# Routing logits brought to token order by 32x32 transposes and four products with a repeated identity

## The chip, the core and the metric

The program runs on one core of one Trainium2 chip. Its engines work side by side and meet through semaphores: TensorE (PE in the rows, its weight loads PEld), VectorE (DVE), ScalarE (ACT), GpSimd (POOL) and SyncE (SP), which here only issues DMAs. The metric is the device time of one execution in microseconds; lower is better. Matrix products write to PSUM, an accumulation memory in banks of 512 fp32 columns on 128 partitions.

## What is computed

Three layers follow each other on a batch of 8 sequences with 576 tokens each. The change lies at the start of the third.

```python
def _attn_ref(q, k, v):              # 8 heads, head size 64, 32 landmarks (means of 18 rows)
    A = sm(q, k_lm); Bm = sm(q_lm, k_lm); C = sm(q_lm, k)
    Z = ...                          # 6 steps of 2 Z - Z Bm Z
    return A @ Z @ C @ v
def _moe_ref(x, w_in, w_out):        # 4608 x 512, 2048 wide
    r = np.maximum(x @ w_in, 0.0)
    return (r * r) @ w_out
def _moe2_ref(x, w_gate, w_output_gate, w1, w2):   # 8 experts, 1024 wide
    logits = x @ w_gate
    e_idx = np.argmax(logits, axis=1)
    probs = softmax(logits); gate_w = probs[arange(N), e_idx]
    eom = 1.0 / (1.0 + np.exp(-(x @ w_output_gate)))
    for e in range(8):
        mask = e_idx == e
        ye = np.maximum(x[mask] @ w1[e], 0.0) @ w2[e]
        out[mask] = gate_w[mask, None] * eom[mask, e, None] * ye
```

## The kernel before

A prologue computes the attention of batch 0 and turns the weights of the second layer into a split form. Then the second layer runs batch by batch (`gemm`), in two halves `c` of HC = 288 tokens. For each of 16 slices `f` of the 2048 hidden columns a hidden block `hp` is made by six products, ACT squares it into a high part `gh` and a square `g`, DVE takes the rest `gl` (`r`, `gh`, `g2`, `gl`, lines 1271 to 1277), and two slices later twelve products add it into four accumulators `acc` (`second`). There is one PSUM bank for `hp`. The attention of the next batch is woven into this stream in small steps (names `bank`, `two`, `x`, `aa`, `ec`, `mb`, `sums`, `st`). After all eight batches the experts of the third layer run (`experts`, names `xs`, `s`, `h`, `y`): in a main pass one expert per batch, the one most of its tokens chose; the other experts that any token chose follow in a loop (`others`).

Between the layers stands the routing, once per batch. `finish` sends the layer's output `x2` to memory and makes the logits. `self.wg` holds the 8 gate and 8 output-gate columns for each of four slices of 128 of the 512 channels, padded to 32. Four products, one per slice `m`, put partial logits into partitions 32m to 32m+31 of one bank `pl`, tokens along the free axis. DVE copies the bank into `lg` (128 partitions x 576 tokens, a half at a time, line 1353). `route` has two steps. `tokens` brings tokens to partitions: six products use 128 (once 64) columns of `lg` as weights and `self.sel` (four 16 x 16 identities stacked) as the moving operand, which adds the four partial sums on the way; five write 16 columns each for the token blocks t = 0 to 4, the sixth repeats the last 128 tokens, so that the 64 tokens of block 4 also stand on partitions 64 to 127. Three DVE copies take this to `L`. Small DVE operations find the largest logit (`oh`, one-hot), ACT takes two exponentials. `counts` multiplies `oh` with ones, in two products (blocks 0 to 3 on 128 partitions, block 4 on 64), to count the tokens of each expert, and derives `prim` and `flags`.

In fp32 each product shows in the trace as two passes: two rows of PE and two of PEld.

The order on each engine is set by a scheduler that simulates the program as it is built: it places every instruction where its model says it can run, with priorities, so a change of lengths moves instructions of other work too. What the code fixes are the calls `after(n, fn)`, which release a step n points of the main stream later, `run_of`, which ties the products of one step together (the products behind the first one get high priority), and `FENCED`, which holds the last logits behind the main stream. Lines 471 to 484 (`matmul`, `big`, `transpose`) are helpers: products of the woven steps appear under line 472 or 484, those of the main stream under 476, those called on the engine directly under their own line. In the prologue all appear under line 104.

Of the kernel before, what the change touches and what calls it, by code (L numbers as in the profile page):

```python
# [9 lines left out]
F32 = mybir.dt.float32  # L10
# [7 lines left out]
ALU = mybir.AluOpType  # L18
AX = mybir.AxisListType
# [3 lines left out]
B, H, S, D = 8, 8, 576, 64  # L23
LM = 32
# [3 lines left out]
NE = 8  # L28
# [4 lines left out]
HC = S // 2  # L33
KD = DM // 128
NFC = FF // 128
NT = (S + 127) // 128
NB = S // LM
# [40 lines left out]
def rows_of(t):  # L78
    return min(128, S - 128 * t)
# [42 lines left out]
class Kernel:  # L122
# [285 lines left out]
    def constants(self):  # L408
# [27 lines left out]
        self.sel = cst.tile([128, 16], F32, name="sel")  # L436
        for h in range(4):
            p = slice(32 * h, 32 * h + 32)
            nc.vector.tensor_copy(out=self.sel[p, :], in_=ident[p, 32 * h:32 * h + 16])
# [891 lines left out]
    def finish(self, b, c, x2):  # L1331
        nc = self.nc
        if c == 0:
            self.lg = self.rp.tile([128, S], F32, tag="lg", name="lg")
# [4 lines left out]
        def logits():  # L1339
# [13 lines left out]
            nc.vector.tensor_copy(out=lg[:, c * HC:(c + 1) * HC], in_=pl[:, 0:HC])  # L1353
# [6 lines left out]
    def route(self, b, lg):  # L1360
# [11 lines left out]
        def tokens():  # L1372
            pt = self.aux.tile([128, 512], F32, tag="b", name="pt")
            for t in range(NT):
                nc.tensor.matmul(  # L1375
                    pt[0:rows_of(t), 16 * t:16 * t + 16], lhsT=lg[:, 128 * t:128 * t + rows_of(t)], rhs=self.sel,
                    start=True, stop=True,
                )

            nc.tensor.matmul(pt[:, 16 * NT:16 * NT + 16], lhsT=lg[:, S - 128:S], rhs=self.sel, start=True, stop=True)  # L1380
            nc.vector.tensor_copy(out=L[64:128, NT - 1, :], in_=pt[64:128, 16 * NT:16 * NT + 16])
            nc.vector.tensor_copy(out=L[:, 0:NT - 1, :].rearrange("p t e -> p (t e)"), in_=pt[:, 0:16 * (NT - 1)])
            nc.vector.tensor_copy(out=L[0:64, NT - 1, :], in_=pt[0:64, 16 * (NT - 1):16 * NT])
# [14 lines left out]
        def counts():  # L1398
# [12 lines left out]
                pc[0:32, 0:NE * (NT - 1)], lhsT=self.ones, rhs=oh[:, 0:NT - 1].rearrange("p t e -> p (t e)"),  # L1411
                start=True, stop=True,
            )
            nc.tensor.matmul(
                pc[0:32, NE * (NT - 1):NE * NT], lhsT=self.ones[0:64, :], rhs=oh[0:64, NT - 1, :], start=True, stop=True
            )
            nc.vector.tensor_reduce(
                out=n[:, 0], in_=pc[0:32, 0:NE * NT].rearrange("p (t e) -> p e t", e=NE), axis=AX.X, op=ALU.add
            )
            nc.vector.tensor_reduce(out=s[:, 0:1], in_=n[:, 0], axis=AX.X, op=ALU.max)  # L1420
# [352 lines left out]
```

## Time and profile before

| quantity | value |
|---|---|
| time, median of 3 runs (lowest to highest) | 1255.96 us (1254.78 to 1258.02) |
| the profiled execution's own time | 1256.76 us |
| its span, first to last instruction | 1254.9 us |
| PE busy | 1217.9 us, 97% |
| DVE, ACT, POOL busy | 606.2, 611.0, 388.9 us |
| mean granted TensorE clock | 0.983 of full speed |

A timeline row reads: start, length, engine, line, operation, output tile <- input tiles, shape of the weights (partitions * columns), shape of the moving operand, and after x the number of passes merged into the row. Lengths of PE rows overlap, because passes are pipelined; what a pass costs the stream is the distance from its start to the start of what follows. The 1.9 us between time and span are outside the program's instructions.

### The profile page before, as it was taken

To read this page: it belongs to the slowest core of one execution; us is meant where nothing else is said; L and a number is where in the kernel's file an instruction comes from. 1 tells how busy PE (TensorE), PEld (TensorE's weight loads), DVE (VectorE), ACT (ScalarE), POOL (GpSimd) and SP (SyncE) were. 2 spreads that over 40 slices of the span, in tenths; PEclk is the share of its full clock that TensorE was granted. 3 is DMA by queue.
4 is the path that set the end of the run, shared out by engine and by line. 5 is a ranking of instruction groups with operands and counts; after the bars stand their busy time and mean duration, and the time that the engine had idled before them with its cause. 6 is when DMAs were issued, how large, how long until landed. Compare 5 with 4: busy or idle time off the path is not lost.

```text
span 1254.9 us, 25184 instructions
## 1 busy us (share of the span) xinstructions
PE 1217.9 (97%) x9886; PEld 1088.7 (87%) x9886; DVE 606.2 (48%) x1522; ACT 611.0 (49%) x1413; POOL 388.9 (31%) x516
## 2 busy tenths in 40 slices
PE   6889899999999999999999999999999999999996
PEld 4679788988988989989989999998898889888885
DVE  7893655755656555645745632234333323323231
ACT  6675355455455565465455454553343433424331
POOL 6540340612432240341341100153342423424220
PEclk8699899999999999999999999999999999999998
DMA  9963043142232142052041220152434435343231
GB/s 332 362 235 113 21 158 115 34 173 77 72 139 77 53 159 77 22 189 73 24 173 40 89 87 1 39 154 82 143 107 137 136 109 160 110 127 108 90 97 40
DMA packets 88408, 142.25 MB, mean 113 GB/s; under 512 B 6430, under 2 KB 61758, under 8 KB 84702
## 3 DMA queue, kind: packets, MB, share of 16 engines
q1 hardware_dynamic: 87854, 139.97, 34.2%
q8 instruction: 80, 1.31, 0.4%
q0 software_dynamic: 288, 0.43, 0.1%
q14 instruction: 42, 0.34, 0.1%
q10 hardware_dynamic: 144, 0.20, 0.0%
HBM read 117.47 MB, written 23.11 MB: 112 GB/s over the span
## 4 chain that ended last, share of the span: by engine, by line
PE 89%; DVE 6%; DMA 2%; ACT 2%; issue 1%; POOL 1%; POOLq 0%; ACTq 0%; DVEq 0%; SPq 0%
PE hp L476 31%; PE acc L476 30%; PE y L476 17%; PE two L472 3%; PE bank L472 2%; DVE x L577 1%; PE bank L484 1%; PE acc L104 1%; DVE sums L104 1%; DMA t<-in_k_dram 1%; PE pl L472 1%; PE bank L104 1%; DMA raw<-in_moe_w_in_dram 1%; PE pt L1375 1%; DMA raw<-in_moe_w_out_dram 0%
## 5 line engine op out<-in xcount | busy, mean ns | idle before, releaser
L476 PE MATMUL acc<-gl,hi 128*128 128x288 f32 x964 | 271.5, 299 | 3.1 <-DVE gl L104 1.6
L476 PE MATMUL acc<-gh,lo 128*128 128x288 f32 x964 | 267.9, 296 | 0.0
L476 PE MATMUL hp<-ab,gb 128*128 128x288 f32 x1434 | 240.3, 302 | 0.2
L476 PE MATMUL y<-s,h 128*128 128x512 f32 (+1 forms) x896 | 223.0, 396 | 0.8 <-ACT h L1518 0.5
L1277 DVE TENSOR_TENSOR gl<-g,gh 128x288 fp32r<-128x288 f32 x224 | 115.4, 516 | 218.0 <-ACT g L1276 216.3
L476 PEld LDWEIGHTS hp<-ab,gb 128*128 128x128 f32 x1434 | 202.1, 189 | 20.8 <-issue 14.7
L476 PEld LDWEIGHTS hp<-xs,s 128*128 128x128 f32 x1536 | 212.2, 188 | 7.4 <-DVE ls L1729 0.3
L476 PE MATMUL hp<-xs,s 128*128 128x288 f32 x1536 | 217.1, 295 | 0.2 <-DVE ls L1729 0.2
L1271 ACT ACTIVATE r<-hp 128x288 f32<-128x288 f32 x224 | 92.0, 411 | 229.0 <-PE hp L476 227.7
L476 PE MATMUL acc<-gh,hi 128*128 128x288 f32 x964 | 196.4, 300 | 0.1
L476 PEld LDWEIGHTS y<-s,h 128*128 128x128 f32 (+1 forms) x896 | 160.6, 184 | 37.7 <-ACT h L1518 0.7
L476 PEld LDWEIGHTS acc<-gl,hi 128*128 128x128 f32 x964 | 181.7, 188 | 10.5 <-DVE gl L1277 2.7
L476 PEld LDWEIGHTS acc<-gh,lo 128*128 128x128 f32 x964 | 181.5, 188 | 0.9 <-issue 0.9
L280 POOL TENSOR_TENSOR s<-r,s 128x256 fp32r<-128x256 f32 x128 | 101.9, 818 | 235.0 <-ACT s L268 234.9
L476 PEld LDWEIGHTS acc<-gh,hi 128*128 128x128 f32 x964 | 149.1, 188 | 18.8 <-ACT gh L1272 11.7
L1518 ACT ACTIVATE h<-hp 128x288 fp32r<-128x288 f32 x128 | 52.6, 411 | 189.0 <-PE hp L476 172.8
L1521 DVE SCALAR_TENSOR_TENSOR h<-hp,h 128x64 fp32r<-128x64 f32 (+2 forms) x192 | 62.6, 354 | 168.5 <-ACT h L1518 168.1
L268 ACT CAST s<-r 128x512 fp32r<-128x512 f32 x128 | 77.6, 617 | 69.3 <-PE y L476 56.3
L1272 ACT ACTIVATE gh<-r 128x288 fp32r<-128x288 f32 x224 | 99.5, 444 | 6.7 <-PE acc L476 0.2
L274 DVE TENSOR_TENSOR s<-r,s 128x512 fp32r<-128x512 f32 x64 | 50.7, 791 | 101.3 <-ACT s L268 101.3
L588 POOL COPY x<-x 32x576 f32<-32x576 f32 x48 | 32.7, 680 | 207.7 <-DVE x L577 108.3
L1276 ACT ACTIVATE g<-r 128x288 f32<-128x288 f32 x224 | 96.0, 429 | 0.0
(267 smaller groups left out, 1350.7 us busy)
## 6 DMA issues: line engine op xcount, KB each, us to landing
r<-in_moe_w_dram SPq DMA_DIRECT2D x128, 256.0 KB
wi<-win SPq DMA_DIRECT2D x28, 1024.0 KB
t<-in_k_dram SPq DMA_DIRECT2D x16, 576.0 KB
t<-in_q_dram SPq DMA_DIRECT2D x16, 576.0 KB
v<-in_v_dram SPq DMA_DIRECT2D x32, 288.0 KB
x_d<-x SPq DMA_DIRECT2D x16, 576.0 KB
xr<-x_d SPq DMA_DIRECT2D x16, 576.0 KB
raw<-in_moe_w_in_dram SPq DMA_DIRECT2D x16, 511.8 KB
```

The costliest lines, as they stand in the source:

```text
L104: return self.kernel.in_lane(self.name, fn(*args, **kw))
L268: hi = self.nc.scalar.copy(out=t[:, 0], in_=raw)
L274: lo_eng.tensor_tensor(out=t[:, 1], in0=raw, in1=t[:, 0].bitcast(F32), op=ALU.subtract)
L280: self.nc.gpsimd.tensor_tensor(out=out[:, p], in0=in0[:, p], in1=in1[:, p], op=op)
L472: self.in_run(lambda: self.nc.tensor.matmul(out, **kw))
L476: mm = self.nc.tensor.matmul(out, **kw)
L1271: nc.scalar.activation(out=r, in_=hp[:, 0:HC], func=ACTF.Relu)
L1272: nc.scalar.activation(out=gh, in_=r, func=ACTF.Square)
L1276: nc.scalar.activation(out=g2, in_=r, func=ACTF.Square)
L1277: nc.vector.tensor_tensor(out=gl, in0=g2, in1=gh.bitcast(F32), op=ALU.subtract)
L1518: nc.scalar.activation(out=h[:, t0:t1], in_=hp[:, 0:HC], func=ACTF.Relu)
L1521: nc.vector.scalar_tensor_tensor(out=h[:, to + a:to + z], in0=hp[:, a - t0:z - t0], scalar=0.0, in1=h[:, a:z].bitcast(F32), op0=ALU.max, o ...
```

## The change

The logits go into `lg` by a DVE transpose of 32 x 32 blocks instead of a copy, so that partition 32m + i of block n holds the 32 padded logit columns of token 32n + i, from channel slice m. Four products then have one and the same weight operand, `self.i32` (four 32 x 32 identities stacked), and stream `lg` with 80 columns each (5 blocks x 16 logits); product q writes the tokens of quarter q of each block of 128 to partitions 32q to 32q+31. They use column tiles of the array, as the four products of `pl` do. One DVE copy takes the result to `L`. `lg` grows to 20 blocks of 32; the last two, which no token fills, are set to zero by POOL once per batch, so that the 64 missing tokens choose expert 0. The counts are then one product over 128 partitions and 40 columns, and a new DVE operation subtracts the 64 (`self.extra`). `self.sel` and its four copies at the start are gone; two memsets of `extra` take their place.

```diff
--- before.py
+++ after.py
@@ -433,10 +433,9 @@
             nc.gpsimd.dma_start(
                 out=self.wg[:, :, NE * j:NE * (j + 1)], in_=w.rearrange("(k p) e -> p k e", p=128)
             )
-        self.sel = cst.tile([128, 16], F32, name="sel")
-        for h in range(4):
-            p = slice(32 * h, 32 * h + 32)
-            nc.vector.tensor_copy(out=self.sel[p, :], in_=ident[p, 32 * h:32 * h + 16])
+        self.extra = cst.tile([32, NE], F32, name="extra")
+        nc.vector.memset(self.extra, 0.0)
+        nc.vector.memset(self.extra[:, 0:1], float(128 * NT - S))
         self.dup = cst.tile([128, 2, D], F32, name="dup")
         for c in range(2):
             p = slice(D * c, D * c + D)
@@ -1331,7 +1330,8 @@
     def finish(self, b, c, x2):
         nc = self.nc
         if c == 0:
-            self.lg = self.rp.tile([128, S], F32, tag="lg", name="lg")
+            self.lg = self.rp.tile([128, NT * 4, LM], F32, tag="lg", name="lg")
+            nc.gpsimd.memset(self.lg[:, NB:], 0.0)
         lg = self.lg
         whole = (b, c) >= FENCED
         late = LOGITS_LATE if b < B - 1 else 2
@@ -1350,7 +1350,10 @@
                         self.follow(mm, e)
             if whole:
                 self.fence, self.fenced = mm, FENCE
-            nc.vector.tensor_copy(out=lg[:, c * HC:(c + 1) * HC], in_=pl[:, 0:HC])
+            n = NB // 2
+            nc.vector.transpose(
+                out=lg[:, n * c:n * c + n, :], in_=pl[:, 0:HC].rearrange("p (n l) -> p n l", l=LM)
+            )
 
         self.after(late, logits)
         if c == 1:
@@ -1371,16 +1374,14 @@
 
         def tokens():
             pt = self.aux.tile([128, 512], F32, tag="b", name="pt")
-            for t in range(NT):
-                nc.tensor.matmul(
-                    pt[0:rows_of(t), 16 * t:16 * t + 16], lhsT=lg[:, 128 * t:128 * t + rows_of(t)], rhs=self.sel,
-                    start=True, stop=True,
-                )
-
-            nc.tensor.matmul(pt[:, 16 * NT:16 * NT + 16], lhsT=lg[:, S - 128:S], rhs=self.sel, start=True, stop=True)
-            nc.vector.tensor_copy(out=L[64:128, NT - 1, :], in_=pt[64:128, 16 * NT:16 * NT + 16])
-            nc.vector.tensor_copy(out=L[:, 0:NT - 1, :].rearrange("p t e -> p (t e)"), in_=pt[:, 0:16 * (NT - 1)])
-            nc.vector.tensor_copy(out=L[0:64, NT - 1, :], in_=pt[0:64, 16 * (NT - 1):16 * NT])
+            with self.run_of():
+                for q in range(4):
+                    self.matmul(
+                        pt[32 * q:32 * q + 32, 0:16 * NT], lhsT=self.i32,
+                        rhs=lg.rearrange("p (t q) l -> p q t l", q=4)[:, q, :, 0:16], start=True, stop=True,
+                        tile_position=(0, 32 * q),
+                    )
+            nc.vector.tensor_copy(out=L.rearrange("p t e -> p (t e)"), in_=pt[:, 0:16 * NT])
             nc.vector.tensor_reduce(out=m[:, 0], in_=L[:, :, 0:NE], axis=AX.X, op=ALU.max)
             nc.vector.tensor_tensor(
                 out=lmx, in0=L[:, :, 0:NE], in1=m[:, 0].unsqueeze(2).to_broadcast(big), op=ALU.subtract
@@ -1408,15 +1409,12 @@
             self.after(2, lambda: nc.sync.dma_start(out=self.rt_d[b], in_=self.rt[:, b]))
             pc = self.aux.tile([128, 512], F32, tag="b", name="pc")
             nc.tensor.matmul(
-                pc[0:32, 0:NE * (NT - 1)], lhsT=self.ones, rhs=oh[:, 0:NT - 1].rearrange("p t e -> p (t e)"),
-                start=True, stop=True,
-            )
-            nc.tensor.matmul(
-                pc[0:32, NE * (NT - 1):NE * NT], lhsT=self.ones[0:64, :], rhs=oh[0:64, NT - 1, :], start=True, stop=True
+                pc[0:32, 0:NE * NT], lhsT=self.ones, rhs=oh.rearrange("p t e -> p (t e)"), start=True, stop=True
             )
             nc.vector.tensor_reduce(
-                out=n[:, 0], in_=pc[0:32, 0:NE * NT].rearrange("p (t e) -> p e t", e=NE), axis=AX.X, op=ALU.add
-            )
+                out=n[:, 3], in_=pc[0:32, 0:NE * NT].rearrange("p (t e) -> p e t", e=NE), axis=AX.X, op=ALU.add
+            )
+            nc.vector.tensor_tensor(out=n[:, 0], in0=n[:, 3], in1=self.extra, op=ALU.subtract)
             nc.vector.tensor_reduce(out=s[:, 0:1], in_=n[:, 0], axis=AX.X, op=ALU.max)
             nc.vector.scalar_tensor_tensor(
                 out=n[:, 1], in0=n[:, 0], scalar=s[:, 0:1], in1=self.desc[0:32], op0=ALU.is_ge, op1=ALU.mult
```

The scheduler places the rest anew. Line numbers of the changed kernel are one or two lower in the helpers (471 for 472, 475 for 476).

On PE, in batch 3, before; `pt` is the routing's result, `two` a bank of the next batch's attention scores, `pc` the counts:

```order
L476 MATMUL acc<-gh,hi 128x288 x4
L1375 MATMUL pt<-sel,lg 128x16 x4
L1375 MATMUL pt<-sel,lg 64x16
L1380 MATMUL pt<-sel,lg 128x16
L472 MATMUL two<-x,lm 32x288 x2
...
L476 MATMUL acc<-gh,lo 128x288
L1410 MATMUL pc<-x,ones 32x32
L1414 MATMUL pc<-x,ones 32x8
L476 MATMUL hp<-ab,gb 128x288 x6
```

The same place in the changed kernel:

```order
L475 MATMUL acc<-gh,hi 128x288 x4
L471 MATMUL pt<-lg,i_122 32x80 x4
L471 MATMUL two<-x,lm 32x288 x2
...
L475 MATMUL acc<-gh,hi 128x288 x4
L1411 MATMUL pc<-x,ones 32x40
L471 MATMUL two<-x,lm 32x288 x6
L475 MATMUL acc<-gl,hi 128x288
```

The counts have moved from the end of an accumulation block to the place in front of the next six score products, some eight large products earlier.

On PE, in batch 2 before, the second half's logits `pl` stand in two pieces:

```order
L476 MATMUL acc<-gh,lo 128x288
L472 MATMUL pl<-x_5046,wg 32x288
L476 MATMUL acc<-gh,hi 128x288
L476 MATMUL acc<-gl,hi 128x288
L476 MATMUL acc<-gh,lo 128x288
L472 MATMUL pl<-x_5046,wg 32x288 x3
```

and in the changed kernel in one:

```order
L475 MATMUL acc<-gh,hi 128x288
L475 MATMUL acc<-gl,hi 128x288
L475 MATMUL acc<-gh,lo 128x288
L471 MATMUL pl<-x_5039,wg 32x288 x4
L475 MATMUL hp<-ab,gb 128x288 x6
```

On POOL, in the changed kernel, while batch 0's second half runs on PE; `st` and `sums` are the means of q and k for a later batch, and the memset is that of batch 1's `lg`:

```order
L529 TENSOR_TENSOR sums<-st 128x128
L529 TENSOR_TENSOR st<-t 128x288 x2
L1334 MEMSET lg 128x64
L529 TENSOR_TENSOR st<-st 128x256
L529 TENSOR_TENSOR st<-st 128x128
L529 TENSOR_TENSOR st<-st 128x64
L529 TENSOR_TENSOR sums<-st 128x128
```

The row of the memset is new between two steps of the second sum; it waits for PE and DVE, since there is one buffer for `lg` and batch 0's `tokens` must have read it.

## Rows read from the trace of the kernel before

**Rows 1.** The page: part 1, busy time by engine; part 4, the chain by engine.

```profile
PE 1217.9 (97%) x9886; PEld 1088.7 (87%) x9886; DVE 606.2 (48%) x1522; ACT 611.0 (49%) x1413; POOL 388.9 (31%) x516
...
PE 89%; DVE 6%; DMA 2%; ACT 2%; issue 1%; POOL 1%; POOLq 0%; ACTq 0%; DVEq 0%; SPq 0%
```

**Rows 2.** One tile's instructions, pt: shortest, median, longest ns; first and last start.

```profile
L1375 PEld LDWEIGHTS pt<-sel,lg x80: 132/192/193, 164.5 to 854.3; 128*128 128x128 f32 x64, 128*64 128x64 f32 x16
L1375 PE MATMUL pt<-sel,lg x80: 177/262/263, 164.6 to 854.4; 128*128 128x16 f32 x64, 128*64 128x16 f32 x16
```

**Rows 3.** Timeline of PE around pt in batch 0 (first) and batch 7 (last).

```profile
164.64 1.18 PE L1375 MATMUL pt<-sel,lg 128*128 128x16 f32 x10
...
165.99 0.38 PE L476 MATMUL acc<-gl,hi 128*128 128x288 f32 x1
166.21 0.29 PE L476 MATMUL acc<-gh,lo 128*128 128x288 f32 x1
...
853.40 1.18 PE L1375 MATMUL pt<-sel,lg 128*128 128x16 f32 x10
...
854.75 2.81 PE L476 MATMUL y<-s,h 128*128 128x512 f32 x11
```

**Rows 4.** Timeline of PE around pt in batch 3, where scores follow.

```profile
471.61 1.18 PE L1375 MATMUL pt<-sel,lg 128*128 128x16 f32 x10
...
473.04 0.68 PE L472 MATMUL two<-x,lm 64*32 64x288 f32 x4
```

**Rows 5.** Timeline of PE around the counts in batch 3.

```profile
480.12 0.29 PE L476 MATMUL acc<-gl,hi 128*128 128x288 f32 x1
480.25 0.29 PE L476 MATMUL acc<-gh,lo 128*128 128x288 f32 x1
480.48 0.25 PE L1410 MATMUL pc<-x,ones 128*32 128x32 f32 x2
...
480.81 1.05 PE L476 MATMUL hp<-ab,gb 128*128 128x288 f32 x6
```

**Rows 6.** Timeline of PE around two blocks of products on column tiles.

```profile
162.59 0.69 PE L472 MATMUL pl<-x,wg 128*32 128x288 f32 x8
163.22 1.06 PE L476 MATMUL hp<-ab,gb 128*128 128x288 f32 x6
...
273.42 0.33 PE L472 MATMUL bank<-lm 64*32 64x32 f32 x16
273.68 0.40 PE L476 MATMUL acc<-gl,hi 128*128 128x288 f32 x1
```

**Rows 7.** Timeline of PE around the split logits of batch 2.

```profile
361.40 0.67 PE L472 MATMUL pl<-x,wg 128*32 128x288 f32 x2
362.00 0.40 PE L476 MATMUL acc<-gh,hi 128*128 128x288 f32 x1
...
362.60 0.69 PE L472 MATMUL pl<-x,wg 128*32 128x288 f32 x6
363.21 0.40 PE L476 MATMUL acc<-gh,hi 128*128 128x288 f32 x1
```

**Rows 8.** DVE: the copy of logits by tile; a transpose of like size, timeline.

```profile
L1353 DVE COPY lg<-pl x16: 419/457/458, 138.9 to 837.6; 128x288 f32<-128x288 f32 x16
...
134.76 0.44 DVE L655 STREAM_TRANSPOSE aa<-two 128x288 f32<-128x288 f32 x1
```

**Rows 9.** Timeline: POOL's sums during batch 0's routing; PE's last use of them.

```profile
158.28 1.79 POOL L530 TENSOR_TENSOR st<-t 128x288 f32<-128x288 f32 x2
...
171.53 0.46 POOL L530 TENSOR_TENSOR sums<-st 128x128 f32<-128x128 f32 x1
...
181.72 0.27 PE L484 MATMUL bank<-ident,sums 128*128 128x128 f32 x1
```

**Rows 10.** DVE's sel copies, timeline; then busy us by engine, clock, DMA share.

```profile
3.81 0.94 DVE L104 COPY sel<-ident 32x16 f32<-32x16 f32 x4
...
0.00:60.00 60.00, 43.07 (x574) 31.81 (x575) 47.55 (x115) 40.22 (x82) 38.84 (x55) 0.74 1.00 347
```

## The prediction

> **What bounds the kernel.** I read the page first. PE is busy 97% of the span, every other engine at most half of it, and PE holds 89% of the chain that ended last [rows 1]. So a microsecond taken from PE's stream should come off the end, unless it opens a wait. A busy share doesn't price an edit on PE, though, since passes overlap. I therefore read the timeline of PE from start to start. In the large products a pass of 288 columns follows the one before after 0.13 us (480.12 to 480.25) [rows 5]. What a small block takes beyond that pace is its cost.
>
> **What the six token products cost now.** They are 80 + 16 passes in the program, twelve per batch, each with only 16 moving columns but with a weight load of 192 ns [rows 2]. In batch 0 they hold the stream from 164.64 to 165.99, 1.35 us, in batch 7 again 1.35 us (853.40 to 854.75) [rows 3]; that is 0.11 us a pass, far more than 16 columns need, so the weight loads set it. In batches 3 to 5, with products on column tiles behind them, it is 1.43 us (471.61 to 473.04) [rows 4]. Batches 1, 2 and 6 read in the same way give 1.35, 1.19 and 1.35. Sum over eight: 10.9 us.
>
> **What the four products will cost.** The trace has no block of this shape: eight passes, four column tiles, 80 columns. Two blocks on column tiles bound it. The four `pl` products (eight passes, two for each tile, 288 columns) hold the stream 0.63 us, 162.59 to 163.22; sixteen passes of 32 columns, four for each tile, hold it 0.26 us, 273.42 to 273.68 [rows 6]. If the tiles work side by side, a block is a fixed part and the columns that one tile streams: 576 in the first, 128 in the second. The difference, 0.37 us for 448 columns, is 0.82 ns a column and leaves 0.15 us fixed. The new block streams 2 x 80 = 160 columns a tile: 0.15 + 0.13 = 0.28 us. In front of a column-tiled block the stream pauses as well: `pc` starts 0.23 us after the pass before it instead of 0.13 [rows 5]. That is 0.37 us together. Bounds: 0.35 from the 32-column block, 0.72 from `pl`. I take 0.37, because the new block is in columns much nearer to the former.
>
> In batches 3 to 5 the order puts `pt` directly in front of `two`, which is column-tiled too, so the pause of 0.1 us, which 1.43 contains already, is paid once, and the block body lies between 0.13 and 0.28; I take 0.2, together 0.3. New sum: 5 x 0.37 + 3 x 0.3 = 2.7 us. **Term 1: 10.9 - 2.7 = 8.2 us gained.**
>
> The row says what changes sides here: today's `pt` follows its neighbour without a pause, since both use the whole array; tomorrow's pays 0.1 us ahead and the fixed 0.15 us behind. The Trainium skill (TensorEngine Tiling (Array Packing), Key Properties) says against this change that changing the tiling mode drains TensorE. `pc` and `pl` agree. Were the switch free, the block would cost 0.13 us, term 1 would be 9.9 us, and the whole sum 1243.4 us.
>
> **The counts.** Today two products: from 480.25 to 480.81 is 0.56 us, 0.43 over the pace [rows 5]. Seven batches are like this or a little dearer apart, batch 7 pays 0.53: 3.5 us. Now one product of 40 columns. Alone (batches 0, 6, 7) it keeps the pause of 0.1 and the first product's 0.18 us (480.48 to the second's start), 0.28 us. In batches 1 to 5 it now stands beside `two`, shares its pause, and adds 0.07 (2 x 40 x 0.82 ns) to 0.18 us; I take 0.1. New sum 3 x 0.28 + 5 x 0.1 = 1.3 us, gain 2.2 us. Behind a small block there is a second hitch one pass on: 165.99 to 166.21 is 0.22 us, 0.09 more than the pace [rows 3]. Six such hitches go with blocks that no longer stand alone (five merged ones, one of batch 0's two): 0.5 us. **Term 2: 2.7 us.**
>
> **The order of the logits.** In batch 2 `pl` stands in two pieces today, 361.40 to 362.00 and 362.60 to 363.21, 0.60 and 0.61 us [rows 7]; with two pauses that is 1.4 us. In one piece it is 0.63 + 0.1 [rows 6]. With one hitch less **term 3 is 0.8 us**.
>
> **What I cost at nothing.** DVE transposes 128 x 288 from PSUM in 0.44 us and copies it in 0.46 us [rows 8]; three small copies become one, and one subtraction on 32 partitions is added. DVE is idle half the time [rows 1], and its next product `gl` stands no later. POOL's eight memsets are a quarter of the size of an `st` step; POOL is idle 69%. One of them brings a wait. In batch 1's place POOL reaches it about 160.1 (158.28 + 1.79) [rows 9] and must wait until batch 0's `pt` has read `lg`, about 165. Behind it stand the rest of the second sum and the third and fourth. The fourth ends at 172.0 today and would end about 177; PE takes it at 181.72 [rows 9], about 180.4 then. The slack of 9.7 us covers it; if a load waits for the delayed sums too, it shrinks further, by up to 5 us, and PE could wait 1.5 us. At the start, `sel`'s four copies leave DVE's chain, 0.94 us. But the DMA queues are full over the first 60 us (share 1.00) [rows 10], and what follows waits for transfers. Bounds 0 to 0.9 gained; I take 0.
>
> The moved work between batches 1 and 5 (score products, transposes, `gl`) has the same operations in another order; its waits may move either way, and I put plus or minus 1.5 us on that.
>
> **Sum.** 8.2 + 2.7 + 0.8 = 11.7 us off the profiled execution's 1256.76 gives 1245.06, so **1245.0 us**. That execution lies 0.8 us above the median of the runs, 1255.96; against the median the sum would be 1244.3.
>
> **Rivals.**
>
> *The products don't run side by side, or the strided moving operand (five runs of 16) slows them.* Eight passes one behind the other are 8 x 80 x 0.82 ns = 0.5 us, with 0.25 us around them about `pl`'s bound of 0.72. Term 1 then loses 8 x 0.35 = 2.8 us: 1247.8. Against it: `pl` with eight passes of 288 columns would need 1.9 us in a row and takes 0.63 [rows 6]. It lies within my range.
>
> *The counts come too early.* `pc` now stands some 5.5 us behind the end of `pt` in batches 1 to 5, in front of `two` and of PE's stream; it needs `oh` from a chain of about ten small DVE operations with a `gl` and a 32-partition transpose in between. I add their lengths to about 4.5 us, so 1 us of slack. If the chain is 2 us longer, PE waits 1 us five times: 1250.
>
> *The gain isn't passed on.* If the woven attention, not PE, paced batches 1 to 5 (transposes on DVE, loads), the saved time would come back as waits there and only batches 0, 6 and 7 would gain, some 1.2 us each: 1253.1, within the noise. Against it: PE's share of 97% and its 89% of the chain [rows 1].
>
> *Slower: ACT meets the routing's exponentials too early.* In batch 1 both exponentials now stand in ACT's queue ahead of a `gb` conversion and of the Relu that empties the only `hp` bank. ACT must wait for DVE's chain; if that runs past the next hidden block's turn, PE stands still, microsecond for microsecond. I work the slack out at about 0.6 us in batch 1. To end 0.3% slower this would have to eat 11.7 + 3.8 us, 3.1 us in each of the five reordered batches; with a slack of 0.6 us it decides only where the chain takes some 3.7 us longer than I add up in each of the five: some 1260 us. The trace shows nothing of that size around today's routing.
>
> **Chances and range.** 0.3% of the median is 3.8 us, about what a measurement can tell from no change, so faster means below 1252.2, slower above 1259.7. My forecast with its bounds (1242 to 1248.5, the first rival within) 0.78; waits that eat 4 to 8 us, as early counts, 0.11; gain not passed on 0.07; slower 0.04. That makes faster 0.89, same 0.07, slower 0.04. The range goes from 1242 (free switching, the 0.9 us at the start, a lucky order) to 1250.5, which takes in early counts.
>
> **What would show it.** In the new profile: `pt` in batch 0 start to start near 0.28 us (0.62 would be the first rival); `pc` at about 0.1 us beside `two`; PE busy about 11 us less, the span shorter by as much; POOL waiting for `pt` some 5 us near 160 with PE not waiting for `sums`; in batches 1 to 5 no PE wait for DVE in front of `pc`. I am wrong if the span shrinks by less than 8 us while `pt` and `pc` cost what I say: then the new order has opened waits, and PE's rows before `acc` or `pc` will name DVE or ACT.

## The result, and the profile after

The changed kernel takes 1245.98 us, median of 4 runs (1245.15 to 1246.25), against 1256.30 us of the kernel before, median of 4 runs: ratio 0.992, 95% interval 0.9907 to 0.9932. The prediction was 1245.0 us with a range of 1242 to 1250.5. The profiled execution's span went from 1254.9 to 1244.2 us.

The page of the changed kernel, busy time by engine and the chain that ended last by engine (they answer to [rows 1]):

```profile
PE 1207.0 (97%) x9838; PEld 1078.3 (87%) x9838; DVE 606.4 (49%) x1512; ACT 610.0 (49%) x1413; POOL 390.0 (31%) x524
...
PE 91%; DVE 5%; DMA 1%; ACT 1%; issue 1%; POOL 0%; POOLq 0%; ACTq 0%; DVEq 0%; SPq 0%
```

PE is busy 10.9 us less and still holds the chain; the other engines' busy times are what they were to about 1 us. The timeline of PE around the token products, in batch 0, batch 3 and batch 7 (compare [rows 3, 4]):

```profile
163.63 0.34 PE L471 MATMUL pt<-lg,i 128*32 128x80 f32 x8
163.91 0.40 PE L475 MATMUL acc<-gl,hi 128*128 128x288 f32 x1
164.15 0.29 PE L475 MATMUL acc<-gh,lo 128*128 128x288 f32 x1
...
465.64 0.35 PE L471 MATMUL pt<-lg,i 128*32 128x80 f32 x8
465.92 0.68 PE L471 MATMUL two<-x,lm 64*32 64x288 f32 x4
...
843.09 0.34 PE L471 MATMUL pt<-lg,i 128*32 128x80 f32 x8
843.37 2.83 PE L475 MATMUL y<-s,h 128*128 128x512 f32 x11
```

The block holds the stream 0.28 us wherever it stands (163.63 to 163.91; 465.64 to 465.92; 843.09 to 843.37), where the six products alone held it 1.35. One pass later there is the hitch: 163.91 to 164.15 is 0.24 us where the pace is 0.13.

The timeline of PE around the counts, in batch 3, where score products follow, and in batch 6, where they stand alone (compare [rows 5]):

```profile
471.50 0.26 PE L1411 MATMUL pc<-x,ones 128*32 128x40 f32 x2
471.69 0.70 PE L471 MATMUL two<-x,lm 64*32 64x288 f32 x12
...
751.25 0.29 PE L475 MATMUL acc<-gh,lo 128*128 128x288 f32 x1
751.48 0.26 PE L1411 MATMUL pc<-x,ones 128*32 128x40 f32 x2
751.66 1.06 PE L475 MATMUL hp<-ab,gb 128*128 128x288 f32 x6
```

Alone, `pc` costs 0.23 + 0.18 - 0.13 = 0.28 us over the pace. Beside the scores it still takes 0.19 us from its start to theirs. And the logits of batch 2 stand in one block (compare [rows 7]):

```profile
359.16 0.69 PE L471 MATMUL pl<-x,wg 128*32 128x288 f32 x8
359.78 1.06 PE L475 MATMUL hp<-ab,gb 128*128 128x288 f32 x6
```

POOL, the timeline while batch 0's routing runs, with the new memset, the last of the delayed sums, and PE's last use of them (compare [rows 9]):

```profile
156.52 0.80 POOL L529 TENSOR_TENSOR st<-t 128x288 f32<-128x288 f32 x1
164.07 0.15 POOL L1334 MEMSET lg<- 128x64 f32 x1 [6.74 <-PE pt L471]
...
174.66 0.46 POOL L529 TENSOR_TENSOR sums<-st 128x128 f32<-128x128 f32 x1
...
179.49 0.27 PE L483 MATMUL bank<-ident,sums 128*128 128x128 f32 x1
```

POOL waits 6.7 us for `pt`, where some 5 were foretold, ends its sums at 175.1, and PE comes for them 4.4 us later.

**An account of PE's stream.** The distances between the starts of successive passes can be sorted without remainder. The stretch runs from the start of batch 0's second logits to the last hidden pass of the experts; it holds 6433 large passes (those of `hp`, `acc` and `y`) in every kernel here. Each is set down at its level (0.133 us, 0.233 for `y`), together 942.8 us. A *block* is what the small products between two large passes add to the level. Of the direct distances, those 60 to 150 ns over the level are *hitches*, those further over are *waits*, and what the rest differs from the level in sum is the *pace*, which can be negative. All in us, with the number of hitches and waits in brackets:

| kernel | stretch | blocks | hitches | waits | pace |
|---|---|---|---|---|---|
| before | 1076.66 | 113.65 | 19.62 (204) | 3.59 (8) | -2.99 |
| changed | 1066.45 | 103.50 | 18.69 (193) | 2.74 (6) | -1.28 |
| difference | -10.21 | -10.15 | -0.93 | -0.85 | +1.71 |

So the small products and what they drag behind them gave back 11.1 us, fewer waits in the new order 0.9, and 1.7 us were lost in something that no step of the prediction held: the large passes themselves run slower by a quarter of a ns each, 0.2%. It isn't the clock: the granted clock is 1.00 over the whole stretch in every run here. The runs below find out what it is.

### The profile page after: what moved, and what is told of

Read it like the earlier page. It is cut to its first block, busy times and chain, and to the rows that moved or that the text cites. A ratio compares the mean times of both kernels' runs of the same rounds, so it can differ in the third digit from the quotient of the medians.

```text
span 1244.2 us, 25082 instructions
## 1 busy us (share of the span) xinstructions
PE 1207.0 (97%) x9838; PEld 1078.3 (87%) x9838; DVE 606.4 (49%) x1512; ACT 610.0 (49%) x1413; POOL 390.0 (31%) x524
## 4 chain that ended last, share of the span: by engine, by line
PE 91%; DVE 5%; DMA 1%; ACT 1%; issue 1%; POOL 0%; POOLq 0%; ACTq 0%; DVEq 0%; SPq 0%
PE hp L475 32%; PE acc L475 31%; PE y L475 17%; PE two L471 4%; PE bank L471 2%; PE bank L104 2%; PE bank L483 1%; DVE x L576 1%; PE acc L104 1%; PE pl L471 1%; DMA raw<-in_moe_w_in_dram 1%; DMA raw<-in_moe_w_out_dram 0%; PE hp L104 0%; DVE lo L104 0%; DVE ma L687 0%
```

## The experiments

Times are medians beside runs of the kernel before on the same chip (1255.5 to 1256.3 us); each kernel's stretch is sorted as above:

| run | time | stretch | blocks | hitches | waits | pace |
|---|---|---|---|---|---|---|
| e4, changed kernel again | 1247.00 | 1066.43 | 103.48 | 18.70 (193) | 2.74 (6) | -1.28 |
| e1, two counts | 1247.32 | 1067.30 | 104.30 | 18.68 (193) | 2.74 (6) | -1.21 |
| e2, `sel` back | 1246.42 | 1067.32 | 103.52 | 18.63 (193) | 2.79 (6) | -0.41 |
| e3, one count alone | 1257.35 | 1077.88 | 113.19 | 19.59 (203) | 2.73 (6) | -0.42 |
| e5, tokens doubled | 1248.34 | 1068.23 | 104.40 | 19.03 (196) | 3.29 (7) | -1.28 |
| e6, more on one tile | 1250.89 | 1071.43 | 107.75 | 18.77 (194) | 3.28 (7) | -1.16 |
| e7, wide counts | 1247.68 | 1066.71 | 102.88 | 19.05 (197) | 3.35 (7) | -1.36 |
| e8, wide counts and tokens | 1247.24 | 1068.15 | 103.70 | 18.75 (196) | 4.31 (12) | -1.40 |
| e9, kept `lg` | 1246.62 | 1066.52 | 103.49 | 18.71 (193) | 2.77 (6) | -1.24 |
| e10, e8 with kept `lg` | 1246.78 | 1067.23 | 103.61 | 18.38 (192) | 3.93 (11) | -1.47 |
| e11, padding | 1244.60 | 1065.13 | 103.53 | 18.63 (193) | 2.82 (6) | -2.64 |
| e12, padding and wide where alone | 1243.86 | 1064.51 | 103.12 | 18.55 (193) | 2.83 (6) | -2.78 |

Blocks, hitches and waits of the changed kernel's two executions agree to 0.02 us, and so does the pace, though the medians of their times lie 1 us apart. The account sees what the times can't: what happens ahead of the stretch and behind it is left out of it.

### e1: two counts in the changed kernel

```diff
-                pc[0:32, 0:NE * NT], lhsT=self.ones, rhs=oh.rearrange("p t e -> p (t e)"), start=True, stop=True
+                pc[0:32, 0:NE * (NT - 1)], lhsT=self.ones, rhs=oh[:, 0:NT - 1].rearrange("p t e -> p (t e)"),
...
+                pc[0:32, NE * (NT - 1):NE * NT], lhsT=self.ones[0:64, :], rhs=oh[0:64, NT - 1, :], start=True, stop=True
```

> The changed kernel with the counts as two products again, over 128 and 64 partitions, and without the subtraction. Theory A, from the account of the two traces block by block (pc costs PE 3.2 us over eight batches before and 1.7 after): some 1.5 us of the gain are the counts, so this run takes about 1247.5 us, and pc alone in front of a hidden block costs 0.42 us over the pace where the changed kernel has 0.28. Theory B, the prediction's second term: the counts bring 2.2 us and hitches another 0.5, so 1248.7 us. If pc costs nothing either way (off the path), 1246.0.

Timeline of PE around the counts of batch 6:

```profile
751.35 0.25 PE L1411 MATMUL pc<-x,ones 128*32 128x32 f32 x2
751.53 0.23 PE L1415 MATMUL pc<-x,ones 64*32 64x8 f32 x2
751.69 1.06 PE L475 MATMUL hp<-ab,gb 128*128 128x288 f32 x6
```

Alone the second product costs 0.15 us, as expected (the two take 0.334 us from 751.35 to 751.69, the one product of the changed kernel 0.189); in front of scores it costs 0.02 (batch 3: its two passes start at 471.53 and 471.58, among those of the scores, which begin at 471.54). The stretch is 0.85 us longer, 0.80 of it in blocks. Both theories put more on the counts as one product: it is worth 0.8 us here, neither 1.5 nor 2.7. The time, 1247.32 us, lies near theory A's 1247.5, but it is only 0.3 us above the changed kernel's beside it (e4) and decides nothing.

### e2 and e4: sel's copies put back, and the changed kernel again

```diff
+        self.sel = cst.tile([128, 16], F32, name="sel")
+        for h in range(4):
+            p = slice(32 * h, 32 * h + 32)
+            nc.vector.tensor_copy(out=self.sel[p, :], in_=ident[p, 32 * h:32 * h + 16])
```

> The changed kernel with the four copies that build sel put back at their old place on DVE, between wg and dup; nothing reads sel. Theory A: the copies delay DVE's first sum of a landed k by 0.6 us and this passes down the chain of the prologue, so the first large product of batch 0 starts near 38.4 us (37.82 in the changed kernel, 38.42 before) and the time is 0.6 us higher, 1246.6. Theory B, the prediction's choice (the start waits for transfers, the copies cost nothing): the first large product stays near 37.8 and the time at 1246.0; then the earlier start seen in the changed kernel was chance of the transfers.

> The changed kernel once more, beside the others on one chip. Theory A (the gain is taken off PE's stream, block by block): 1246.0 within 0.5 us, the first large product near 37.8 us, the last product starting about 11.3 us sooner than before, with the rest of the difference to the span (0.6 us) in the last transfers to memory, which vary from run to run. Rival: the start's 0.6 us varies by chance, then the first large product moves by some tenths here.

DVE's first sum over a landed `k`, and PE's first large product of batch 0, timeline; of the changed kernel, of e4 and of e2:

```profile
4.64 2.20 DVE L104 TENSOR_REDUCE sums<-t 128x32 f32<-128x576 f32 x2 [0.21 <-DMA t<-in_k_dram]
...
37.82 2.42 PE L104 MATMUL hp<-ab,gb 128*128 128x288 f32 x5 [1.22 <-ACT gb L104]
```

```profile
4.78 2.20 DVE L104 TENSOR_REDUCE sums<-t 128x32 f32<-128x576 f32 x2 [0.34 <-DMA t<-in_k_dram]
...
38.69 1.33 PE L104 MATMUL hp<-ab,gb 128*128 128x288 f32 x2 [0.98 <-ACT gb L104]
```

```profile
5.24 1.15 DVE L104 TENSOR_REDUCE sums<-t 128x32 f32<-128x576 f32 x1
...
38.51 1.92 PE L104 MATMUL hp<-ab,gb 128*128 128x288 f32 x3 [1.70 <-ACT gb L104]
```

Without `sel` the first sum does start sooner, 4.64 and 4.78 against 5.24, though it waits 0.21 and 0.34 us for its transfer. By the first large product nothing of it is left: 37.82 and 38.69 without the copies, 38.51 with them. Theory A of e2 fell; the 0.6 us that the first pair of traces seemed to show were chance. The prediction's zero for the start holds. e4's time, 1247.00 us, misses what was expected of it (1246.0 within 0.5), while its stretch is the changed kernel's to 0.02 us. But e2's stretch is 0.9 us longer than e4's with the same blocks, hitches and waits: all of it is pace, and the kernel differs by nothing but a tile of 64 bytes a partition and its four copies in the first 6 us.

### e3: one count, without the new tokens

```diff
-            nc.vector.tensor_copy(out=L[64:128, NT - 1, :], in_=pt[64:128, 16 * NT:16 * NT + 16])
+            nc.vector.memset(L[64:128, NT - 1, :], 0.0)
...
-                pc[0:32, 0:NE * (NT - 1)], lhsT=self.ones, rhs=oh[:, 0:NT - 1].rearrange("p t e -> p (t e)"),
...
-                pc[0:32, NE * (NT - 1):NE * NT], lhsT=self.ones[0:64, :], rhs=oh[0:64, NT - 1, :], start=True, stop=True
...
+                pc[0:32, 0:NE * NT], lhsT=self.ones, rhs=oh.rearrange("p t e -> p (t e)"), start=True, stop=True
...
+            nc.vector.tensor_tensor(out=n[:, 0], in0=n[:, 3], in1=self.extra, op=ALU.subtract)
```

> The kernel before, with its copy into lg, its six token products and sel, but the counts as one product over 128 partitions: the repeated tokens on partitions 64 to 127 of block 4 are overwritten by zeros (a DVE memset in place of that copy), and the subtraction is added. Theory A: only the counts gain, 1.2 to 1.5 us, so about 1254.9 us against 1256.3; pt still costs 1.35 us over the pace. Theory B, the prediction's second term: 2.7 us, 1253.6. Should this run gain far more than 3 us, the gain of the change is not in the token products.

The cut leaves out the tile `extra` and its two memsets, which stand beside `sel` here. This run missed both theories: 1257.35 us is 0.13% slower than before (ratio 1.0013, 1.0004 to 1.0022). Against the kernel before, the counts' own blocks cost 0.9 us less, other blocks 0.5 more where the order moved them, and two waits go with 0.86: 1.3 us, what theory A asked for, though not all from the counts. Then the pace loses 2.57 us, and the sum is 1.2 us worse. The token products cost what they did before, so the gain of the change does lie in them. And the pace moved again, in another kernel that holds one more small tile.

### e5 and e6: is it side by side?

e5 issues each token product twice on its own tile, behind the first four and with the same operands:

```diff
+                for q in range(4):
+                    self.matmul(
+                        pt[32 * q:32 * q + 32, 128:128 + 16 * NT], lhsT=self.i32,
...
+                        tile_position=(0, 32 * q),
```

e6 puts the four additional ones on the first tile:

```diff
+                        pt[0:32, 128 + 80 * q:128 + 80 * q + 16 * NT], lhsT=self.i32,
...
+                        tile_position=(0, 0),
```

> The changed kernel with the four token products issued twice in each batch, the second time into unused columns of the same bank, on the same four column tiles; the output is the same. Theory A (the four tiles stream side by side, a block is 0.15 us fixed plus 0.82 ns for each column that one tile streams): pt holds PE 0.276 us today, then 160 columns more a tile, 0.13 us: 0.41 us, 1.05 us more over eight batches. Rival (the passes follow one another and today's 0.276 us is eight passes in a row): 0.55 us or more.

> The changed kernel with four more token products in each batch, all four on the first column tile, into unused columns of the same bank; the output is the same. Theory A (side by side across tiles, one behind the other on one tile): the first tile streams 640 columns more, 0.52 us at 0.82 ns, so pt holds PE 0.276 + 0.52 = 0.80 us and the run is 4.2 us longer. Rival (no tile works beside another): the same 0.55 us as with the products spread over four tiles, and the same time.

Timeline of PE in batch 6, e5 and then e6:

```profile
748.77 0.48 PE L471 MATMUL pt<-lg,i 128*32 128x80 f32 x16
749.18 0.41 PE L475 MATMUL acc<-gl,hi 128*128 128x288 f32 x1
```

```profile
751.40 0.88 PE L471 MATMUL pt<-lg,i 128*32 128x80 f32 x16
752.21 0.40 PE L475 MATMUL acc<-gl,hi 128*128 128x288 f32 x1
```

Eight passes more cost 0.138 us (0.414 against 0.276) when they are spread over four tiles and 0.534 us (0.81) when they stand on one. That is 0.86 and 0.83 ns for each column of the busiest tile; the prediction took 0.82 from two blocks of other shapes. Side by side is shown, and the first rival is out. Side by side doesn't mean four times the rate, though: on the whole array a pass of 288 columns takes 0.133 us, 0.46 ns a column, so four tiles side by side stream about 2.2 columns in the time of one on the whole array, not four (an estimate from these figures). The stretch rose by more than the blocks, 1.8 and 5.0 us against 1.1 and 4.3 in `pt`: the scheduler placed other work anew, with one wait of 0.5 us more in each.

### e7 and e8: small products on the whole array

e7 gives the counts 128 columns of ones as weights:

```diff
-        self.ones = cst.tile([128, 32], F32, name="ones")
+        self.ones = cst.tile([128, 128], F32, name="ones")
...
-                pc[0:32, 0:NE * NT], lhsT=self.ones, rhs=oh.rearrange("p t e -> p (t e)"), start=True, stop=True
+                pc[:, 0:NE * NT], lhsT=self.ones, rhs=oh.rearrange("p t e -> p (t e)"), start=True, stop=True
```

e8 also makes the four token products one (`i128` is the 32 x 32 identity four times down and four times across):

```diff
+            nc.tensor.matmul(
+                pt[:, 0:64 * NT], lhsT=self.i128.rearrange("p h l -> p (h l)"), rhs=lg[:, :, 0:16], start=True, stop=True
+            )
+            for q in range(4):
+                p = slice(32 * q, 32 * q + 32)
+                nc.vector.tensor_copy(
+                    out=L[p], in_=pt[p, 0:64 * NT].rearrange("p (t q e) -> p q t e", q=4, e=16)[:, q]
+                )
```

> The changed kernel with the counts' weights widened from 32 to 128 columns of ones, so that the product uses the whole array (128 x 128 weights, 40 columns moving). Theory A (the pause ahead of pc and the 0.19 us behind its start come from the change of tiling): pc starts 0.13 us after the pass before it instead of 0.22, and its two passes cost 0.11 us each, as the old token products did, so 0.22 us over the pace instead of 0.28; in the four batches where score products follow, these pay the pause themselves, and the sum over eight batches is within 0.3 us of today's: the time stays at the changed kernel's. Rival (the pause is a wait for oh from DVE, whatever the tiling): 0.22 us ahead of pc as today.

> As the run with the wide counts, and the four token products become one: weights of 128 x 128 (the 32 x 32 identity repeated four times down and four times across), all 320 columns of lg moving; every quarter of the partitions then holds all tokens, and four DVE copies of 32 partitions each pick the right ones instead of one copy. Theory A (the change of tiling costs 0.1 us ahead and some 0.1 behind): two passes of 320 columns at 0.148 us, no pause, 0.30 us over the pace against 0.37, so 0.5 us off the eight batches; DVE's chain to oh grows by about 0.5 us, which the distance to the counts covers. Rival 1: the moving operand in runs of 16 columns streams slower than a plain one, pt costs over 0.4 us. Rival 2: the longer chain makes PE wait in front of pc, then up to 0.5 us in five batches, 2.5 us.

Timeline of PE in batch 6, the counts in e7 and then the token product in e8:

```profile
753.06 0.29 PE L475 MATMUL acc<-gh,lo 128*128 128x288 f32 x1
753.19 0.31 PE L1411 MATMUL pc<-x,ones 128*128 128x40 f32 x2
753.33 0.65 PE L475 MATMUL hp<-ab,gb 128*128 128x288 f32 x3
```

```profile
751.25 0.70 PE L1379 MATMUL pt<-lg,i 128*128 128x320 f32 x2
751.55 0.54 PE L477 MATMUL acc<-gl,hi 128*128 128x288 f32 x1
751.93 0.30 PE L477 MATMUL acc<-gh,lo 128*128 128x288 f32 x1
```

In e7 `pc` follows at the pace, 0.13 us after the pass before it, and costs 0.14 us over the pace (0.22 was expected) where the column tile cost 0.28, with a smaller hitch (0.083 against 0.105). So the pause of 0.1 us comes from the change of tiling and not from a wait for `oh`: the rival fell, and what the prediction took from the Trainium skill (TensorEngine Tiling (Array Packing), Key Properties), that changing the tiling mode drains TensorE, agrees with this pair of runs. Beside scores it saves little, for these then pay the pause (`pc` to `two` 0.24 us instead of 0.19; in batch 3 `pc` and `two` together cost 0.87 us over the pace instead of 0.91). Over the program blocks gain 0.6 us; four hitches and one wait of 0.5 us more, from other places, take it back.

In e8 the block costs 0.30 us over the pace, as expected, but the pass behind the next comes 0.38 us later (751.55 to 751.93), a hitch of 0.24 us. Block and hitch are 0.54 us against 0.367 + 0.105 for the four products, and in front of scores (batches 3 to 5) 0.63 us pass from `pt` to `two` instead of 0.28. The stretch is 1.7 us longer than the changed kernel's, where theory A had 0.5 us less. Rival 2 fell: `pc` follows the pass before it at the pace in all eight batches. Whether the runs of 16 columns stream slower, or the next weights come later, the trace doesn't tell. The four products on tiles are the better form here.

### e9 and e10: no memset, no wait of POOL

```diff
-        if c == 0:
+        if b == c == 0:
             self.lg = self.rp.tile([128, NT * 4, LM], F32, tag="lg", name="lg")
             nc.gpsimd.memset(self.lg[:, NB:], 0.0)
```

> The changed kernel with one lg for the whole program, its last two blocks set to zero once at batch 0, so that POOL has no memset in batches 1 to 7 and no wait for pt (40.7 us in the changed kernel's waits of POOL). Theory A, the prediction's (the wait is harmless, PE never waits for sums through it): the time stays within 0.5 us of the changed kernel, and PE's account from the second logits to the last expert product stays at 1066.4 us plus or minus 1. Rival: POOL's delay holds transposes or loads back, then 1 to 1.5 us less here and fewer waits of PE for eu (2.2 us).

> Wide counts, the one token product and the kept lg together. If each has its price as stated (0.5 us for the token product, nothing for the other two), 0.5 us less than the changed kernel, which the times can hardly tell from no change; the account of PE's stream can: some 1066 us from the second logits to the last expert product against 1066.4. Rival: PE waits in front of pc for the longer chain on DVE, 1 to 2.5 us more.

POOL's 40.7 us of waiting for `pt` are gone from its waits in e9, and PE's stretch is 1066.52 us against 1066.45: the wait was harmless. e10 is e8 with this: it carries e8's large hitches (five of its eleven entries under waits are 0.24 us each) and lies 0.8 us above the changed kernel in the stretch. That is the rival's direction, but not its cause: PE doesn't wait in front of `pc`, which follows the pass before it at the pace in every batch.

### e11 and e12: where the pace comes from

e11 changes no instruction: in every engine's order it is the changed kernel. `extra` takes 64 bytes a partition in SBUF, as `sel` did, instead of 32. e12 adds 128 columns of ones (512 bytes) and uses them for the counts of batches 0, 6 and 7.

```diff
-        self.extra = cst.tile([32, NE], F32, name="extra")
+        self.extra = cst.tile([32, 16], F32, name="extra")[:, 0:NE]
...
+                pc[0:32 if 0 < b < 6 else 128, 0:NE * NT], lhsT=self.ones if 0 < b < 6 else self.wide,
```

The last line is e12's alone; its tile `wide` and the memset of it are left out.

> The changed kernel with extra made 16 columns wide instead of 8 (64 bytes a partition, as sel was, instead of 32), so that all that lies behind it in SBUF stands where it stood before the change; every engine's order of instructions is the changed kernel's. In the traces so far the mean pace of large passes that follow each other undisturbed differs by some tenths of a ns, and is the same, form by form, in kernels with the same displacement: a gl pass to a gh pass 131.44 ns before, 133.15 and 133.14 in the changed kernel's two traces, 132.67 and 132.67 in the two kernels that hold sel and extra. Theory A (the pace goes by the address): 131.4 ns here, the expert passes' and the others' as before, some 1.7 us less from the second logits to the last expert pass (1066.4 now, 1064.7 here), and a time near 1244.8 us. Theory B (the pace is chance of the execution or the chip): 133.1 or anything else, 1066.4 us and 1246.5.

> The same, and in batches 0, 6 and 7, where the counts stand alone among large passes, the counts' weights are 128 columns of ones (another 512 bytes a partition). With counts over the whole array pc alone cost 0.14 us over the pace and a hitch of 0.083, against 0.28 and 0.105 on a column tile. Theory A: 0.17 us less in each of three batches, 0.5 us from the second logits to the last expert pass against the run with the padding alone, if the 512 bytes leave the pace as it is. Rival: the pace goes by the address with a longer period, then all passes change by tenths of a ns again and the 0.5 us can't be seen.

The timeline of PE at the ends of the stretch and at the last logits (batch 7), of the kernel before (its start is the first row of [rows 6]), of the changed kernel, and of e11:

```profile
836.81 0.69 PE L472 MATMUL pl<-x,wg 128*32 128x288 f32 x8
...
1239.39 5.75 PE L476 MATMUL y<-s,h 128*128 128x512 f32 x24
```

```profile
161.49 0.69 PE L471 MATMUL pl<-x,wg 128*32 128x288 f32 x8
...
826.40 0.69 PE L471 MATMUL pl<-x,wg 128*32 128x288 f32 x8
...
1228.06 5.78 PE L475 MATMUL y<-s,h 128*128 128x512 f32 x24
```

```profile
159.53 0.69 PE L471 MATMUL pl<-x,wg 128*32 128x288 f32 x8
...
823.34 0.69 PE L471 MATMUL pl<-x,wg 128*32 128x288 f32 x8
...
1224.79 5.75 PE L475 MATMUL y<-s,h 128*128 128x512 f32 x24
```

From logits to logits the changed kernel takes 664.91 us and e11, with the same instructions in the same order, 663.81; to the start of the last `y` block 1066.57 and 1065.26 (the expectations and the table stop one pass earlier). Blocks, hitches and waits are the same within 0.1 us. Form by form the pace is back where it was before: a `gl` pass to the next `gh` pass takes 131.44 ns on average before (832 pairs), 133.15 in the changed kernel, 131.77 in e11; a `y` pass to the next 233.18, 233.75 and 233.19; and in e2 and e3, which hold both small tiles, a hidden pass of the experts takes 133.25 and 133.27 where it takes 132.51 before and after. Theory A stands: the pace goes by where the tiles lie. Chance of the chip, theory B, doesn't explain it: e1, e2, e3 and e4 ran on one chip, and their paces are -1.21 and -1.28 without `sel`, -0.41 and -0.42 with `sel` and `extra`; six traces of kernels with `extra` alone, from three chips or more, lie between -1.16 and -1.28. e11 and e12 were traced once each, on a chip that has no trace of another layout; the kernel before took 1256.01 us there, as on the others.

The padding regained 1.36 of the 1.71 us (1064.7 us was expected for the stretch, 1065.13 measured); the other 0.35 stay open. `lg` still takes 256 bytes a partition more than before, so not everything need stand where it stood. 1244.60 us is 1.4 and 2.4 us under the two medians of the changed kernel, though these were timed on other occasions; beside the kernel before it is 11.4 us less, where the changed kernel was 10.3 and 8.5 less. Which tile, and what about its address matters, no run here separates. One regularity stands in the traces: 512 bytes more (e11 to e12, e7 to e8) leave every form with over 100 pairs as it was within about 0.2 ns, `gl` to `gh` for example at 131.77 and 131.56, and at 132.92 and 132.94, while 32 bytes more (the changed kernel to e11) or 384 more (to e7) change the forms by up to 1.4 ns.

e12's counts cost 0.14 us with a hitch of 0.086 in the three batches, 0.5 us in all, and the stretch is 0.6 us shorter than e11's. Its time, 1243.86 us (ratio to before 0.9902, 0.9886 to 0.9917), is the lowest median of the study; between e11 and e12 the times alone could not decide. The profiled execution of e12 is even its slowest, 1246.81 us: its stretch starts at 164.51, 5.0 us later than e11's, and ahead of it (141.3 to 148.1) the granted clock stood at 0.50, the level of 1.2 GHz, after a wait of PE of 1.6 us, while in e11 it was 1.00 from 60 us to the end of the stretch.

## Why the prediction was right, step by step

**What bounds the kernel** was read rightly: 10.9 us less PE work gave 10.3 us less time (8.5 when it was timed again, e4), and in sum none of it came back as waits for other engines. The third and fourth rivals didn't come about: PE's waits in the stretch fell from 3.59 to 2.74 us, and none of them is for an exponential.

**Term 1, the token products,** was priced at 8.2 us. Measured: 11.2 us before, hitches included, and 3.2 after, 8.0 us. The block itself was forecast at 0.28 us from two blocks of other shapes and measured 0.276. One step in it was off by a little: beside `two` I took 0.2 us for the block body; the block takes its 0.276 there too. The two blocks share the pause and nothing else.

**Term 2, the counts,** was priced at 2.7 us and is the mis-sized one: it measured 2.0. Block by block with hitches the counts cost 4.1 us before and 2.1 after. I had set down batch 2 before at 0.4 us, where the second product hid among scores and the two cost 0.19 together; batch 7 at 0.53, where 0.43 are left once the pass in front of the counts, a `y`, is taken at its own level of 0.233; and in the new place I took 0.1 us for each of five batches, where it is 0.19, by the same error as in term 1. Of the six hitches five go, since batch 2's was shared with scores already; 0.5 us is right even so. And only 0.8 of the 2.0 us belongs to the single product (e1); 1.2 come from standing beside scores, which is the scheduler's doing.

**Term 3, the logits in one block,** 0.8 us, measured 0.8: 0.694 + 0.708 with two hitches before, 0.714 with one after.

**The moved work** was given plus or minus 1.5 us around zero; it brought 0.9 us in two waits fewer. The kernel before waited in batch 3 for a `gl` that directly followed a hidden block, timeline of PE, kernel before:

```profile
404.56 1.06 PE L476 MATMUL hp<-ab,gb 128*128 128x288 f32 x6
405.99 0.40 PE L476 MATMUL acc<-gl,hi 128*128 128x288 f32 x1 [0.37 <-DVE gl L1277]
```

In the changed kernel the same `gl` comes behind other products and doesn't wait. e3, e5, e6 and e7 show that such waits come and go with other edits too.

**What was costed at nothing** cost nothing: POOL's wait (e9), the start (e2 and e4), and DVE's steps, which no new wait of PE names (no run varies them). The counts, moved forward, didn't wait either, so the second rival was rightly out.

**What no step held** is the pace, 1.7 us lost. At the pace of the kernel before the stretch would have gained 11.9 us, against 11.7 forecast. The loss is larger than the 1.0 us by which the time lies above the forecast.

**What was luck.** The three terms measured 8.0 + 2.0 + 0.8 = 10.8 us, not 11.7; that 11.9 comes so near is mostly owed to the waits, 0.9 us, which the prediction held at zero. And 1245.0 was taken off an execution that lies 0.5 us above the median of the kernel before, 1256.30; against the median the forecast would have been 1244.6, and the miss 1.4 us instead of 1.0. In the profiled pair two accidents also lie outside the stretch and partly cancel. Behind the start of the last `y` block the program took 0.6 us longer. The stretch's start came 1.1 us sooner (162.59 and 161.49). Between 60 us and there the granted clock fell once to 0.50 in each, for 6.8 us before (139.2 to 146.0) and for 3.4 after (152.6 to 156.0), with large passes 0.24 us apart in place of 0.13. PE had just waited, 1.6 us before, 0.6 and 0.4 us after; e11 has all of these waits and no such fall.

## What to carry to other kernels

On an engine that is the bound, price a small block by distances from start to start, with the pause ahead of it and the hitch one pass behind it, and fit a fixed part and a slope from two blocks that stand on the same column tiles; here that hit 0.276 us with 0.28. A block on column tiles costs a pause of 0.09 us to enter wherever it stands alone. So the counts are cheapest beside other tiled products (0.19 us) or, where they must stand alone, on the whole array (0.14 and a hitch of 0.08, instead of 0.28 and 0.105). That doesn't hold for every small product: the 320 columns of e8 cost more on the whole array than on four tiles. Before a result of a few tenths of a per cent is put down to an edit, sort the distances of both traces: here 32 bytes of padding moved the stretch by 1.3 us, more than the counts as one product did (0.8).

## What the runs showed that I had not expected

- The pace of large passes depends on the layout of SBUF, not on chance: two executions of the changed kernel agree to 0.01 us in 6433 passes, and kernels with other displacements differ by up to 2.6 us over the stretch (-2.99 to -0.41), with each form of pass moving its own way. The granted clock is 1.00 over the stretch in all of them.
- A product of 64 rows and 8 columns costs PE 0.15 us behind another one of the counts and 0.02 us when its passes start among those of 64-row score products (e1).
- One product with 320 moving columns in runs of 16 costs 0.30 us and then a hitch of 0.24 us where others have 0.08 to 0.11 (e8).
